# Three matmuls into an unread PSUM bank, ahead of the down projection of a one-token attention and gated MLP block

## The chip, the cores and the metric

The kernel runs on one core of a Trainium2 chip. The metric is device time in microseconds (us). The kernel before took 656.71 us, the median of three runs (656.64 to 656.9).

## What is computed

One token (512 values) passes through a layer norm, a grouped-query attention over a cache of 65,536 positions (32 query heads, 8 key/value heads of 128 values), a residual sum, a second layer norm, a gated MLP of width 1792 and a second residual sum. All inputs are bf16.

```python
q = layernorm(x) @ wq                          # 32 heads of 128
p = softmax(q . k_cache * 128**-0.5)           # 65536 positions, 4 query heads per kv head
h = x + (p . v_cache) @ wo                     # 4096 -> 512
n = layernorm(h)
h2 = h + (sigmoid(n @ w_gate) * (n @ w_up)) @ w_down   # 512 -> 1792 -> 512
```

The two caches are 268 MB of the 282.33 MB that the profile shows as read.

## The kernel before, in words

The program is written out by hand for each engine: `op(engine, function, waits, name)` appends one instruction to the list of its engine, and `emit` gives each name that somebody waits for a semaphore count. An instruction of a list runs behind all those ahead of it in the same list; what is not in `waits` is not waited for. An `op` without a name and without waits, as in the diff, neither waits nor raises a semaphore.

The cache streams through SBUF (`ring`) in large DMAs, all issued by SyncE (SP) in one order: for each of the eight heads a piece of K, a piece of V, and so on; then `w_o`, the last pieces of V, `w_gate`, `w_up`, and last `w_down` in three pieces (rows 0 to 8, 9 to 12, and 13 of fourteen, L362 to L365). VectorE (DVE) transposes the K blocks (L522), TensorE (PE) makes the scores and the sums over V (L434), ScalarE (ACT) the exponentials (L568).

After the last head comes a tail with one operation behind another:

- PE L641 makes the last four rows of the output projection in columns, DVE L824 adds `x` to give `hT`, and L392 to L404 with PE L395 make the mean and the reciprocal deviation (`rstd`, GpSimd L406).
- DVE L825 makes `hc`, the centred column; DVE L827 makes `hz`, from which the residual is put back into a row later.
- PE L838 multiplies `hc` by `w_gate` and `w_up`: 32 matmuls with one column of weights, 448 moving columns each, four beside one another in strips of 32 columns of the array, into the PSUM banks GB (2) and UB (3).
- PE L843, the residual's matmul, writes `h` into the bank YB (5) and opens the sum there. Its operands are fp32, and the trace shows it as two records.
- ACT L845 (tanh), DVE L846, L848 and L851 make the gated values `hh` and their transpose `hhT`.
- PE L857 adds the product with `w_down` to YB: fourteen rows of four matmuls with 128 columns, each group of four in the four strips. The first matmul of each piece waits for that piece's DMA (`wd0`, `wd1`, `wd2`), the very first one for `hhT` too.
- DVE L861 and ACT L862 copy the result out, and two DMAs (L865, on SP and ACT) write it to HBM.

PSUM bank PO is number 4. The heads' sums over V are made in it; ACT L609 reads it for the last time at the end of the last head. `ident` is a 128x128 identity in bf16, made at the start. `ktw` holds transposed K blocks, later rows of `w_o`; its first 384 columns are rows of `w_o` at the place of the change.

The wait of the down projection:

```python
["hhT", "hhT0", f"wd{i}"] if r == r0 and g == 0 else ()
```

Of the kernel before, what the change touches and what calls it, by code (L numbers as in the profile page):

```python
# [29 lines left out]
PO = 4  # L30
# [5 lines left out]
class Prog:  # L36
# [14 lines left out]
    def op(self, eng, fn, deps=(), name=None, to=None, times=1):  # L51
        assert name is None or name not in self.where, name
        self.ops[eng].append(dict(fn=fn, deps=[d for d in deps if d], name=name, dma=None, to=to, times=times, part=self.part.get(eng)))
        if name:
            self.where[name] = (eng, len(self.ops[eng]) - 1)
# [160 lines left out]
def bass_sequential_preLN__gqa_block_cached__glu_gated_glu__decode_kernel(  # L216
# [22 lines left out]
    with ExitStack() as es:  # L239
        def sb(name, shape, dt):  # L240
            return es.enter_context(nc.sbuf_tensor(name, shape, dt))
# [7 lines left out]
        ident = sb("ident", [128, 128], bf16)  # L249
# [7 lines left out]
        ktw = sb("ktw", [128, NKT * CH + WH], bf16)  # L257
# [48 lines left out]
        def ps(bank, c0, c1, p0=0, p1=128):  # L306
            return PS[p0:p1, bank * 512 + c0: bank * 512 + c1]
# [5 lines left out]
        op, dma = P.op, P.dma  # L313
# [519 lines left out]
        for i, (nm, bank) in enumerate((("wg", GB), ("wu", UB))):  # L833
            at = W_AT[nm]
            for kt in range(4):
                for c in range(4):
# [3 lines left out]
                        rhs=ring[:, at + kt * FF + c * FG: at + kt * FF + (c + 1) * FG],  # L840
                        start=(kt == 0), stop=(kt == 3), tile_position=(0, 32 * c)),
                       ["hc"] * (kt == 0 and c == 0) + dep, f"gu{i}" if kt == 3 and c == 3 else None)
        op("pe", lambda e: e.matmul(ps(YB, 0, 128), lhsT=gsel[:, :], rhs=hz[:, :], start=True, stop=False, skip_group_check=True), ["hz"])  # L843

        op("act", lambda e: e.activation(sg[:, :], ps(GB, 0, FG), AF.Tanh, scale=rstd[1][:, 0:1]), ["gu0", "rstd.1"], "sg")  # L845
        op("dve", lambda e: e.tensor_scalar(sg2[:, :], sg[:, :], 1.0, rstd[1][:, 0:1], op0=ALU.add, op1=ALU.mult), ["sg"], "sg2")  # L846
# [5 lines left out]
        for i, (r0, r1) in enumerate(WD_SPLIT):  # L852
            for r in range(r0, r1):
                for g in range(4):
# [4 lines left out]
                        start=False, stop=(r == NF - 1), tile_position=(0, 32 * g), skip_group_check=True),  # L859
# [36 lines left out]
```

## Time and profile before

| | |
|---|---|
| time, median of 3 runs (lowest, highest) | 656.71 us (656.64, 656.9) |
| time of the profiled execution | 656.72 us |
| its span, first to last instruction | 655.4 us |
| mean granted TensorE clock | 0.783 |
| busy: PE, DVE, ACT | 397.5, 350.5, 43.1 us |
| DMA queue of SP, share of 16 engines | 99.6% |
| read from HBM | 282.33 MB, 431 GB/s over the span |

Busy times overlap, so they do not add up to the span. The row of the DMA queue says that the 16 DMA engines had packets of it under way nearly throughout. The granted clock is the share of full speed that TensorE's clock gate let through; 0.5 and 1 are the two values it takes here over a stretch. A granted clock of one stretch comes from the view that cuts the span into windows.

### The profile page before, as it was taken

What the parts mean: (1) busy time and instruction counts of PE and PEld (TensorE: products, weight loads), DVE (VectorE), ACT (ScalarE), POOL (GpSimd) and SP (SyncE); (2) the same over time, 40 slices, a digit from 0 to 9 for tenths busy, and PEclk for the clock granted to TensorE, in tenths of its full rate; (3) what the DMA queues carried; (4) which work ended last, traced back from release to release, by engine and by line L of the source; (5) the groups of instructions that cost most, each with busy time, mean ns of one, the idle gap of its engine ahead of it and who ended that gap; (6) DMA issues with size and microseconds to landing.
All of it is one profiled execution on the core that took longest, in us unless ns stands there. A gap on an engine that the chain in (4) does not pass through costs nothing.

```text
span 655.4 us, 6173 instructions
## 1 busy us (share of the span) xinstructions
PE 397.5 (61%) x2317; PEld 66.0 (10%) x1549; DVE 350.5 (53%) x426; ACT 43.1 (7%) x114; POOL 3.6 (1%) x18
## 2 busy tenths in 40 slices
PE   2788672937548393764828467383855728285465
PEld 1100010110101000010100101010010101001122
DVE  3398853819266290935719184481917548092202
ACT  1100200020000200002000200002000020001101
POOL 1000000000000000000000000000000000000000
PEclk9789795877959587795968869596786969778656
DMA  9999999999999999998999999999999989999998
GB/s 390 442 432 464 424 408 448 448 436 396 448 448 448 424 408 448 448 448 384 448 448 448 428 404 448 448 448 408 424 448 448 448 384 448 448 448 424 427 404 361
DMA packets 6376, 282.33 MB, mean 431 GB/s; under 512 B 744, under 2 KB 872, under 8 KB 1256
## 3 DMA queue, kind: packets, MB, share of 16 engines
q1 hardware_dynamic: 6340, 282.33, 99.6%
q10 hardware_dynamic: 36, 0.00, 0.0%
HBM read 282.33 MB, written 0.00 MB: 431 GB/s over the span
## 4 chain that ended last, share of the span: by engine, by line
DMA 66%; DVE 31%; PE 1%; issue 1%; SPq 0%; PEldq 0%
DMA ring<-in_A_k_cache_dram 58%; DVE ktw L522 31%; DMA ring<-in_B_w_down_dram 5%; DMA ring<-in_A_v_cache_dram 4%; PE PS L434 1%; SPq L359 0%; PE PS L857 0%; SPq L364 0%; SPq L330 0%; DVE y_sb L861 0%; PEldq L171 0%
## 5 line engine op out<-in xcount | busy, mean ns | idle before, releaser
L522 DVE STREAM_TRANSPOSE ktw<-ring 128x1024 f32<-128x1024 f32 x256 | 291.7, 1208 | 166.6 <-DMA ring<-in_A_k_cache_dram 166.6
L434 PE MATMUL PS<-ktw 128*128 128x512 bf16 x1024 | 278.0, 421 | 163.4 <-DVE ktw L522 156.0
L434 PE MATMUL PS<-ring,PT_sb 128*32 x1024 | 85.7, 423 | 54.3 <-issue 46.2
L434 PEld LDWEIGHTS PS<-ktw 128*128 x256 | 26.2, 103 | 403.7 <-issue 240.3
L609 ACT ACTIVATE po_sb<-PS,rl 128x512 bf16<-128x512 f32 x8 | 5.5, 687 | 524.4 <-PE PS L434 524.4
L434 PEld LDWEIGHTS PS<-ring,PT_sb 128*32 x1024 | 20.7, 116 | 117.5 <-issue 116.1
L557 DVE TENSOR_REDUCE gmj<-PS 1x4 f32<-1x128 f32 x8 | 2.2, 279 | 53.3 <-PE PS L555 53.3
L529 DVE TENSOR_REDUCE M_sb<-PS 128x1 f32<-128x512 f32 x32 | 19.9, 683 | 19.3 <-PE PS L434 19.3
L568 ACT ACTIVATE P_sb<-PS,negmax 128x512 bf16<-128x512 f32 x32 | 21.5, 685 | 0.3
L578 DVE STREAM_TRANSPOSE PT_sb<-P_sb 128x512 bf16<-128x512 bf16 x32 | 19.9, 675 | 1.7 <-ACT P_sb L568 1.7
L434 PE MATMUL PS<-ktw,xz 128*8 x32 | 8.4, 429 | 3.6 <-DMA ktw<-in_A_wq_dram 3.6
L625 DVE TENSOR_TENSOR Lw<-O,blk_of 128x896 bf16<-128x896 bf16 (+1 forms) x2 | 1.4, 682 | 15.9 <-ACT O L615 15.9
L562 PE MATMUL PS<-one_f,gmrep 1*128 1x1 f32 x16 | 4.2, 332 | 5.0 <-DVE gmrep L559 5.0
L555 PE MATMUL PS<-identf,gm 128*1 128x128 f32 x16 | 4.3, 364 | 4.9 <-issue 2.8
L634 DVE CAST O<-PS 128x28 bf16<-128x28 f32 (+1 forms) x2 | 0.3, 173 | 12.7 <-PE PS L631 12.7
L480 DVE STREAM_TRANSPOSE qt<-qh 32x512 bf16<-32x512 bf16 x1 | 0.7, 700 | 11.1 <-ACT qh L477 11.1
L568 ACT ACTIVATION_READ_ACCUMULATOR P_sb<-PS,negmax 128x1 f32 x32 | 6.5, 203 | 0.0
L612 PE MATMUL PS<-sel_bf,po_sb 128*128 128x4 bf16 x32 | 2.1, 170 | 6.3 <-ACT po_sb L609 6.3
L495 ACT ACTIVATE PS<-zcol 128x512 f32<-128x512 bf16 x8 | 5.0, 622 | 0.0
L564 ACT ACTIVATE negmax<-PS 128x1 f32<-128x1 f32 x8 | 1.4, 171 | 54.5 <-PE PS L562 54.5
L583 PE MATMUL PS<-L_sb,lsel 128*128 128x4 f32 x16 | 2.5, 229 | 3.8 <-DVE PT_sb L578 3.8
L415 PE MATMUL PS<-xs,xpick 16*128 16x32 bf16 x1 | 0.2, 203 | 7.4 <-DMA xs<-in_A_x_dram 7.4
(88 smaller groups left out, 67.5 us busy)
## 6 DMA issues: line engine op xcount, KB each, us to landing
ring<-in_A_k_cache_dram SPq DMA_DIRECT2D x4, 4096.0 KB, 35.0
ring<-in_A_v_cache_dram SPq DMA_DIRECT2D x1, 5120.0 KB, 30.0
ktw<-in_A_wq_dram SPq DMA_DIRECT2D x1, 4096.0 KB, 12.2
ktw<-in_A_wo_dram SPq DMA_DIRECT2D x1, 3584.0 KB, 18.3
ring<-in_A_v_cache_dram SPq DMA_DIRECT2D x1, 3072.0 KB, 36.8
ring<-in_B_w_gate_dram SPq DMA_DIRECT2D x1, 1792.0 KB, 23.8
ring<-in_B_w_up_dram SPq DMA_DIRECT2D x1, 1344.0 KB, 26.6
ring<-in_B_w_down_dram SPq DMA_DIRECT2D x1, 1152.0 KB, 29.6
```

The source lines that it names most:

```text
L434: return e.add_instruction(mybir.InstMatmult(name=nc.get_next_instruction_name(), engine=mybir.EngineType.PE, ins=[rhs, lhsT], outs=[e.low ...
L495: op("act", lambda e: e.activation(ps(PO, 0, 512), bass.AP(tensor=zcol, offset=0, ap=[[1, 128], [0, 512]]), AF.Copy), ["zcol"] if h == 0 e ...
L522: op("dve", lambda e, d=dst, sr=src: e.transpose(d, sr), deps, f"T{b}.{c}", to="T")
L529: op("dve", lambda e, u=u: e.tensor_reduce(M_sb[:, u % 4:u % 4 + 1], ps(u % NS, 0, 512), AX.X, ALU.max), [f"S{b}.{NC - NR + k}"], f"mx{u}" ...
L555: op("pe", lambda e: e.matmul(ps(MISC, 0, 128, 0, 1), lhsT=gm[:, :], rhs=identf[:, :], start=True, stop=True), [f"gm{h}"], f"gmT{h}", to="Q")
L557: op("dve", lambda e: e.tensor_reduce(gmj[:, :], ps(MISC, 0, 128, 0, 1).rearrange("p (i a c) -> p a i c", a=4, c=NC), AX.XY, ALU.max), [f" ...
L562: op("pe", lambda e: e.matmul(ps(MISC, 128, 129), lhsT=gmrep[0:1, :], rhs=one_f[0:1, 0:1], start=True, stop=True), [f"gmrep{h}"], f"neg{h}")
L568: op("act", lambda e, b=b: e.activation(P_sb[:, (b % 4) * 512:(b % 4 + 1) * 512], ps(b % NS, 0, 512), AF.Exp, bias=negmax[:, k:k + 1], sca ...
L578: op("dve", lambda e, b=b: e.transpose(PT_sb[:, (b % 4) * 512:(b % 4 + 1) * 512], P_sb[:, (b % 4) * 512:(b % 4 + 1) * 512]), [f"E{b}"], f" ...
L583: op("pe", lambda e: e.matmul(ps(MISC, 132, 136), lhsT=lsel[:, :], rhs=L_sb[:, :], start=True, stop=True), [f"PT{NR * h + NR - 1}"], f"l{h ...
L609: op("act", lambda e: e.activation(po_sb[:, :], ps(PO, 0, 512), AF.Copy, scale=rl[:, :]), [f"PV{h}.{NR - 1}", f"rl{h}"], f"po{h}", to="po")
L612: op("pe", lambda e, t=t: e.matmul(ps(OX, 0, 4), lhsT=po_sb[:, t * 128:(t + 1) * 128], rhs=sel_bf[:, 8 * t:8 * t + 8:2], start=(t == 0), s ...
```

## The change

Behind the residual's matmul (L843), three more matmuls are appended to PE's list, each with the identity as weights (128x128) and 384 columns of `ktw` as moving data, written to columns 0 to 383 of bank PO. Nothing reads the bank afterwards. They have no waits and no names. All else stands as before, with line numbers from L845 on higher by two.

```diff
         op("pe", lambda e: e.matmul(ps(YB, 0, 128), lhsT=gsel[:, :], rhs=hz[:, :], start=True, stop=False, skip_group_check=True), ["hz"])
+        for _ in range(3):
+            op("pe", lambda e: e.matmul(ps(PO, 0, 384), lhsT=ident[:, :], rhs=ktw[:, 0:384], start=True, stop=True, skip_group_check=True))
 
         op("act", lambda e: e.activation(sg[:, :], ps(GB, 0, FG), AF.Tanh, scale=rstd[1][:, 0:1]), ["gu0", "rstd.1"], "sg")
```

In the order of PE's instructions the only difference is one row, three matmuls of 128x384 between L843 and the first matmul of L857; DVE, ACT, GpSimd and SP keep theirs.

## The prediction, as it was put on record

> **What bounds the kernel now.** I read the chain of waits first, over the last 70 us, because the change sits in the last 6 us of the span.
>
> ```profile
> by line: DMA ring<-in_B_w_down_dram 54.2%; DMA ring<-in_A_v_cache_dram 44.3%; PE PS L434 11.6%; issue 5.5%; SPq L359 2.1%; PE PS L857 1.0%; SPq L364 0.8%; DVE y_sb L861 0.5%; PEldq L171 0.3%
> ...
> 622.80 30.34 DMA ring<-in_B_w_down_dram
> 653.15 0.04 issue
> 653.19 0.56 PE PS L857 x17
> 653.75 0.02 issue
> 653.78 0.28 DVE y_sb L861
> ```
>
> The end is set by a DMA: the second piece of w_down, issued at 622.80, lands at 653.15, and 0.04 us later PE does the rest of the down projection. None of gate, up, tanh or transpose is on this chain. Next the instructions in order of time around the change:
>
> ```profile
> 650.30 0.58 PE L843 MATMUL PS<-hz,gsel 128*128 128x128 f32 x2
> 650.42 0.92 DVE L848 TENSOR_TENSOR hh<-PS,sg 128x448 bf16<-128x448 f32 x1 [0.37 <-PE PS L838]
> 651.37 0.65 DVE L851 STREAM_TRANSPOSE hhT<-hh 128x448 bf16<-128x448 bf16 x1
> 652.07 0.51 PEld L857 LDWEIGHTS PS<-ring,hhT 128*32 128x32 bf16 x36 [1.38 <-DVE hhT L851]
> 652.07 0.68 PE L857 MATMUL PS<-ring,hhT 128*32 128x128 bf16 x36 [1.19 <-DVE hhT L851]
> 653.19 0.40 PEld L857 LDWEIGHTS PS<-ring,hhT 128*32 128x32 bf16 x20 [0.61 <-DMA ring<-in_B_w_down_dram]
> 653.19 0.53 PE L857 MATMUL PS<-ring,hhT 128*32 128x128 bf16 x20 [0.43 <-DMA ring<-in_B_w_down_dram]
> ```
>
> PE has two holes here: 1.19 us from the residual's matmul (650.30 + 0.58 = 650.88) to the first row of w_down, ended by hhT, and 0.43 us between the first 36 matmuls and the last 20, ended by the DMA. The three pieces are issued at 622.33, 622.80 and about 623.3; with the 29.6, 30.3 and 30.2 us to landing that the DMA view gives (shortest, longest, median) they land near 651.9, 653.15 and 653.5. So the last row, too, waits for data: the last matmul starts at 653.5 by the line's view and ends at 653.75.
>
> Last the granted clock, from the view by windows (columns: window, length, then busy us and count for PE, weight load, DVE, ACT and POOL, then the clock, DMA share, GB/s):
>
> ```profile
> 650.40:650.50 0.10, 0.10 (x1) 0.10 (x2) 0.08 (x1) 0.00 (x0) 0.00 (x0) 0.50 1.08 461
> 650.50:650.60 0.10, 0.10 (x1) 0.10 (x2) 0.10 (x1) 0.00 (x0) 0.00 (x0) 0.86 1.52 645
> 650.60:650.70 0.10, 0.10 (x2) 0.09 (x1) 0.10 (x1) 0.00 (x0) 0.00 (x0) 1.00 0.87 369
> 650.70:652.00 1.30, 0.19 (x2) 0.00 (x0) 1.27 (x2) 0.00 (x0) 0.00 (x0) 1.00 0.93 386
> 652.00:653.70 1.70, 1.19 (x56) 0.84 (x56) 0.02 (x1) 0.00 (x0) 0.00 (x0) 1.00 0.55 210
> ...
> 653.90:654.00 0.10, 0.00 (x0) 0.00 (x0) 0.10 (x1) 0.10 (x1) 0.00 (x0) 0.71 0.00 0
> ```
>
> The clock goes from 0.50 to 1.00 inside the residual's matmul (0.86 on average in that tenth: at 650.53) and back at 653.94 (0.71: 42% of that tenth still at 1). All of w_down already runs at 1.00 in this execution. The column of GB/s says the rest: the stream runs near 400 GB/s until w_down is in.
>
> **The change part by part.** It removes nothing and moves no DMA, no wait and no other engine's instruction. It adds three weight loads of 128x128 bf16 and three matmuls of 384 columns behind L843, in the 1.19 us hole.
>
> Weight load: 0.103 us by the group of L434's loads of the same shape; the later two can lie beside the matmul ahead of them.
>
> Matmul at clock 1.00: thirteen 128x512 matmuls of L434 stand in 2.98 us from 127.50 (that stretch is at 1.00), and one of them takes 0.377 us on the mean, so one follows another after (2.98 - 0.38)/12 = 0.217 us. For 384 columns that is 0.163. The array is then taken for 0.10 + 3 x 0.163 = 0.59 us: from 650.88 to 651.47, or 0.60 before w_down starts at 652.07. Cost on the path: 0.
>
> Matmul at clock 0.50: the weight loads of L838 come in fours at 647.92, 648.29, 648.66, 649.04, one four per 0.373 us of 448 columns; 384 columns give 0.32, so 0.10 + 0.96 = 1.06 us, to 651.94. That still ends 0.13 us ahead of hhT. Cost: 0.
>
> What if the cover is smaller than this? Behind the three stands only L857 on PE; nobody but the two copies out of YB waits for it. If the first row were late, it would be late by nothing up to 0.43 us, the second hole, at clock 1.00. With all three exposed the ends are: 0.59 - 0.43 = 0.16 us at clock 1.00; at 0.50, 1.06 us less a hole of which w_down at half clock leaves 0.16 (nine fours at 0.373 x 128/448 = 0.107 us are 0.96 us, to 653.03, against 653.19), so 0.9. I take 0, because both rows put the end of the three ahead of hhT.
>
> Effect on DVE's L848 and L851, which run beside the three: they read banks 3 and SBUF, the three write bank 4. The trace shows PE running beside DVE at many places, not this pair. A slow-down of the two (1.57 us) by a quarter would be 0.39 us and stay inside the 0.43; a gain there would be worth nothing, since the DMA ends later. I take 0.
>
> Effect on the clock: w_down at 1.00 cannot become faster. At 0.50 it would end later: the second piece's four fours run from 653.19 to 653.62, the last row's to 653.73, plus the 0.21 us by which a matmul of L838 (0.58) outlasts its spacing (0.373): 653.94 against 653.75, so 0.19 us. That is all that a clock can give or take here: 0 to 0.19 us, 0.03% of the time.
>
> A rule that bears on this: "TensorE: Matmul & The Clock Gate" in the Trainium skill (Part 1, The HAM clock gate) says that about 3.4 us of sustained work release the full clock, that the window of activity is free-running, and that an idle window takes the clock away again. The trace agrees with the length: 653.94 - 650.53 = 3.41 us at 1.00. By that rule fill-in matmuls are worth something where a gap lets the clock fall; here the 0.19 us above is the most it can be.
>
> **The sum.** 656.72 (profiled time) + 0 = 656.72; the profiled execution stands 0.01 above the median, so I predict 656.7. What lies around the span (656.72 - 655.4 = 1.3 us) is not touched.
>
> **The rivals.**
>
> 1. **The clock was lower in other executions, and the three raise it.** Where the switch to 1.00 falls against the kernel can differ between executions. Full work on PE runs from 647.22 to 650.88 now, 3.66 us; with the three it runs to 651.47 or 651.94, 4.25 to 4.7 us, so a stretch of 3.41 us fits in at more positions. If the median execution of before had w_down at 0.50, it would gain 0.19: 656.5. Against it: the profiled execution had 1.00 and took 656.72, the median. For it: the highest run is 656.9, 0.18 above. It would not reach 0.2%.
>
> 2. **Slower: PE's instructions come late.** Six more instructions move the 112 of w_down back in PE's stream. If the sequencer has to wait for code somewhere in them, PE stands idle with no wait to show for it. The longest gap of matmuls of L434 that ends in "issue" is 1.3 us; a stall of that size behind 653.19 is all exposed and gives 658.0, and ahead of 652.07 or in the 0.43 us hole it is hidden for that much: it decides from the point where it outlasts the hole. Against it: the tail from 644.6 on is straight code, and PE's waits from 643 to the end name no "issue" gap at all. "Runtime: NRT & Kernel Launch" in the Trainium skill (Instruction fetch mechanics) says that an engine's code is refilled in blocks of 256 instructions and that crossing into one is mostly hidden; no row here shows a crossing, and by that rule the sum would stay as it is.
>
> 3. **Slower a little: the clock is at 0.50 and the three lie on the path.** Half clock and hhT ready earlier than 651.94, or weight loads that do not overlap (3 x 0.103 in place of one: +0.21, so 652.15, 0.08 us past hhT). With the 0.19 above: 657.0. It is inside 0.2%.
>
> 4. **The stream runs at another rate.** The program is another one, and 282.33 MB at 431 GB/s set the time; a rate off by 0.3% gives 654.7 or 658.7. The three runs of before lie within 0.26 us, 0.04%, which speaks against it.
>
> That the three are not there at all, or stand elsewhere, is ruled out by the order of PE's instructions; if they cost nothing, the time cannot tell.
>
> **How the numbers follow.** A measurement of this kernel can tell about 0.2%, 1.3 us, from no change: 655.4 to 658.0. Chances: no change (656.45 to 656.95) 0.80; rival 1 (656.5) 0.06; rival 2 (658.0) 0.06, of which 0.04 over the bound; rival 3 (657.0) 0.03; rival 4 0.05, 0.02 faster and 0.03 slower. So faster 0.02, same 0.91 (0.80 + 0.06 + 0.02 + 0.03), slower 0.07. Range 656.3 to 657.2: below, the clock's 0.19 under the lowest run (656.64) is 656.45, and I leave 0.15 for a median of few runs; above, rival 3 with the 0.19 that the highest run lies over the median. The fully exposed 0.9 us at half clock and rivals 2 and 4 (0.11) are left out.
>
> **What would show it.** In the profile after: three records of L845 starting at 650.9 after L843 and ending by 651.6 (clock 1.00) or near 652.1 (0.50); the first row of w_down still ended by hhT, 0.05 us after it; a hole ended by DMA w_down ahead of the last 20; the same 0.6 us from the landing to the last matmul. Wrong would be: w_down's first row following the three without a gap while the DMA's hole is gone, an "issue" gap inside L859, w_down at 0.50 throughout, or a landing later than 31 us after its issue.

## The result and the profile after

| | before | after |
|---|---|---|
| median (lowest to highest, 6 runs each) | 656.81 us (656.35 to 657.08) | 660.24 us (660.09 to 660.69) |
| profiled execution | 656.72 us | 660.19 us |
| its span | 655.4 us | 655.4 us |
| time less span | 1.3 us | 4.8 us (4.8 to 5.3 in the six runs) |

After to before is 1.0053, 95% interval 1.0042 to 1.0063: slower by 3.4 us, outside the range. The span has not changed at all. All of the loss lies outside the span, ahead of the first instruction or behind the last.

The profile's first lines for the kernel after: six records more (three loads, three matmuls), the same span.

```profile
span 655.4 us, 6179 instructions
## 1 busy us (share of the span) xinstructions
PE 396.2 (60%) x2320; PEld 67.0 (10%) x1552; DVE 350.3 (53%) x426; ACT 43.1 (7%) x114; POOL 3.6 (1%) x18
```

The instructions of the kernel after in order of time, around the change (start, us, engine, line, operation, count, idle before):

```profile
650.32 0.80 PE L843 MATMUL PS<-hz,gsel 128*128 128x128 f32 x2
...
650.91 1.17 PE L845 MATMUL PS<-ktw,ident 128*128 128x384 bf16 x3
...
652.09 0.88 PEld L859 LDWEIGHTS PS<-ring,hhT 128*32 128x32 bf16 x36 [0.71 <-DVE hhT L853]
652.09 1.65 PE L859 MATMUL PS<-ring,hhT 128*32 128x128 bf16 x56
653.20 0.40 PEld L859 LDWEIGHTS PS<-ring,hhT 128*32 128x32 bf16 x20 [0.23 <-DMA ring<-in_B_w_down_dram]
653.80 0.27 ACT L864 ACTIVATE y_sb<-PS 33x128 bf16<-33x128 f32 x1 [4.21 <-PE PS L859]
```

This execution had clock 0.50 through the three matmuls and w_down up to 653.0, and 0.89 on average from there to 653.8; w_down ended 0.02 us later than before all the same (ACT's copy starts at 653.80, before at 653.78). The loads of the last 20 still wait for the DMA.

### The profile page after: what moved, and what is told of

It reads as the page before. It is cut to its first block, busy times and chain, and to the rows that moved or that the text cites. A ratio compares the mean times of both kernels' runs of the same rounds, so it can differ in the third digit from the quotient of the medians.

```text
span 655.4 us, 6179 instructions
## 1 busy us (share of the span) xinstructions
PE 396.2 (60%) x2320; PEld 67.0 (10%) x1552; DVE 350.3 (53%) x426; ACT 43.1 (7%) x114; POOL 3.6 (1%) x18
## 4 chain that ended last, share of the span: by engine, by line
DMA 63%; DVE 31%; PE 4%; issue 1%; SPq 0%; ACT 0%
DMA ring<-in_A_k_cache_dram 58%; DVE ktw L522 31%; DMA ring<-in_A_v_cache_dram 6%; PE PS L434 2%; PE PS L838 0%; PE PS L859 0%; PE PS L845 0%; SPq L330 0%; PE PS L843 0%; PE PS L641 0%; ACT po_sb L609 0%; PE PS L395 0%; SPq L349 0%; DVE Lw L625 0%; DVE y_sb L863 0%
## 5 line engine op out<-in xcount | busy, mean ns | idle before, releaser
L434 PE MATMUL PS<-ring,PT_sb 128*32 x1024 | 84.2, 416 | 55.5 <-issue 46.9
```

The costliest lines, as they stand in the source:

```text
L434: return e.add_instruction(mybir.InstMatmult(name=nc.get_next_instruction_name(), engine=mybir.EngineType.PE, ins=[rhs, lhsT], outs=[e.low ...
```

## The experiments

My first theory: PE's program got longer by six instructions, and somewhere outside the span PE waits for code (A). The rival: what the three matmuls do (columns, bank, clock) costs something outside the span (B).

**Work or length.** `tiny3` puts three matmuls of one column in the same place, `mm1` and `mm2` one and two of 384 columns, `no_row8` keeps all three and drops a row of w_down's product.

```diff
# tiny3
+        for _ in range(3):
+            op("pe", lambda e: e.matmul(ps(PO, 0, 1, 96, 97), lhsT=zcol[:, :], rhs=zcol[:, :], start=True, stop=True, tile_position=(0, 96), skip_group_check=True))
# mm1, mm2: as the change, with range(1) and range(2)
# no_row8: the change, and in the loop of L859
+                if r == 8:
+                    continue
```

> Before, with three matmuls of one column and one weight column (zeros, 128x1) in place of the three of 384 columns: the same six instructions more on PE, next to no work in the array. Theory A (the 3.4 us are paid outside the span because PE's program got longer, whatever the instructions do): about 660.2. Theory B (the 3.4 us come from what the big matmuls do: 384 columns, a dirtied bank, a clock left in another state at the end): about 656.8. The span is 655.4 by both.

> One matmul of 384 columns in place of three, two instructions more on PE than before. Theory A, if the cost is a step at some length of the program: either 656.8 or 660.2, nothing between. Theory B, or a cost per instruction: about 658.0, a third of 3.4 us more than before.

> Two matmuls of 384 columns, four instructions more on PE. Theory A with a step: 656.8 or 660.2, and no less than with one matmul. Theory B, or a cost per instruction: about 659.1.

> The changed kernel with its three matmuls, but with the ninth row of w_down's product left out (part of the output sum is missing): eight PE instructions fewer, so two fewer than before the change. Theory A: back to 656.8, within 0.2. Theory B: 660.2, since the three matmuls still run.

| run | PE instructions against before | time, us (lowest to highest) | time less span |
|---|---|---|---|
| no_row8 | -2 | 656.69 (656.36 to 657.03) | 1.3 |
| before, same chip | 0 | 656.78 (656.48 to 657.14) | 1.3 |
| mm1 | +2 | 657.05 (656.68 to 657.56) | 1.6 to 1.7 |
| mm2 | +4 | 660.03 (659.83 to 660.59) | 4.4 to 5.0 |
| tiny3 | +6 | 660.37 (660.2 to 660.79) | 4.8 to 5.3 |

B falls twice: one-column matmuls cost as much as 384 columns (tiny3), and the three big ones cost nothing once the program is shorter (no_row8). It is a step in the length between +2 and +4. At +2 the time itself cannot be told from before (ratio 1.0003, interval 0.9993 to 1.0012), but time less span is 0.3 us longer: 1.60 to 1.68 in its ten runs, 1.28 to 1.38 in the nineteen of before.

**Which side of the span, and the branch hint.** All of PE's list stands in a body with a hint at its head and a branch back to the head at its end that is never taken (L179 to L192, `HINTED`). `late_before` and `late_after` add 5.4 us of DVE work behind PE's last matmul; `nohint_before` and `nohint_pad` take PE out of `HINTED`, which removes the hint and the never-taken branch together; below, "without the hint" means without both.

```diff
# late_before, late_after
+        for i in range(8):
+            op("dve", lambda e: e.transpose(hhT[:, 32:32 + FG], hh[:, :]), [f"late{i - 1}" if i else "y"], f"late{i}")
-        op("dve", lambda e: e.tensor_copy(y_sb[0:33, :], ps(YB, 0, 128, 0, 33)), ["y"], "ysb0")
+        op("dve", lambda e: e.tensor_copy(y_sb[0:33, :], ps(YB, 0, 128, 0, 33)), ["late7"], "ysb0")
# nohint_before; nohint_pad besides with range(5) in the change
-HINTED = ("pe", "dve", "act")
+HINTED = ("dve", "act")
```

> The kernel before, with eight more transposes of 128x448 on DVE, one behind the other, between the last matmul and DVE's copy of the result (about 8 x 0.65 to 0.7 us, so the span becomes some 5.5 us longer, about 661). PE has been done for that long when the program ends. Both theories on where the 3.4 us lie: time less span stays 1.3 us; this is the other half of the next run.

> The changed kernel with the same eight transposes. Theory End (PE waits for code at the end of its own program, behind its last matmul, and the program's end waits for PE): PE can do that beside the transposes, so time less span falls from 4.8 to 1.3 us and the time equals that of the kernel before with the transposes. Theory Start (the code is brought in ahead of the first instruction, or all engines are held): time less span stays 4.8 and the time is 3.4 us above it.

> The kernel before without the branch hint and the never-taken branch back around PE's program (PE is taken out of HINTED; three real instructions fewer). Theory Hint (the hint is what brings back the first code block in time, and the longer program defeats it): time less span rises to about 4.8, the time to 660.2. Theory Length alone (only the count decides): 656.8.

> Without the hint, and with five of the 384-column matmuls in place of three, so that PE's program is as long as the changed kernel's. Theory Hint: about 660.2, the same as without hint and short. Theory Length alone: 660.2 too, but 3.4 us above the short one without hint.

Measured: late_before 661.98 (span 660.6, time less span 1.3 to 1.4), late_after 665.64 (span 660.5, 4.7 to 5.1): PE's 5 us of leisure do not hide the cost, so theory End in this form falls. Without the hint the short program takes 657.93 and the long one 657.72, both with time less span 1.3: no step. Both theories that I had written down there fall, too; it takes the length and the hinted branch together. The hinted branch is worth having where the program is short: without it the short one is 1.1 us slower (657.93 against 656.87, ratio 1.0015, interval 1.0006 to 1.0025), all of it in the span (656.2 to 657.0 over ten runs, 655.0 to 656.1 with it over eighteen).

**Which place counts.** Three ways of lengthening, and a stretch of code long enough to bring the place where the step arises, a boundary in the code, into the program itself (`extra` is the one-column matmul of tiny3):

```diff
# behind2 (late_behind20: range(20), with late_before's transposes), behind the hinted branch
             self.nc.switch_bb(end)
+            if e == "pe":
+                for _ in range(2):
+                    self.extra(eng)
# head2, near the head of PE's list
+        for _ in range(2):
+            op("pe", lambda e: e.matmul(ps(PO, 0, D // XR), lhsT=xpick[:, :], rhs=xs[:, :], start=True, stop=True))
# mm2_pull: mm2, and ahead of the hint's target
+            if e == "pe":
+                o = self.ops[e].pop(0)
+                put(e, eng, o, waits_of(e, o, {}, {}, False))
```

> The kernel before with two one-column matmuls (four instructions) behind the never-taken hinted branch, at the very end of PE's program: the program is as long as the one with two 384-column matmuls (660.0), but the body between the hint's target and the branch is as long as before. Theory End place (what decides is where PE's last code, and what the runtime runs after it, comes to lie): 660.0 to 660.4. Theory Branch (what decides is where the hinted branch stands, or how long the body is): 656.8.

> Two small matmuls (32 columns, four instructions) near the head of PE's list, 640 us ahead of the tail, where PE waits for data; all later code moves up by four instructions. Theory Length or place of any kind inside the body: 660.0 to 660.4. If it were the tail's own code that matters: 656.8.

> The kernel with two 384-column matmuls (660.0), with PE's first matmul and its waits moved ahead of the hint's target: the body is as short as with one matmul or shorter, the program's length, the place of the branch and of the end unchanged. Theory Body length (distance from the branch back to its target): 656.8 to 657.1. Theory place or length of the whole: 660.0.

> The kernel before with the eight late transposes on DVE and twenty one-column matmuls (40 instructions) behind the hinted branch at the end of PE's program, where PE has some 5 us until the program ends. If the boundary that is passed lies within these 40 instructions, PE waits for code there beside DVE's transposes. Theory End place with an exposed wait only behind the common end: time less span 1.4, time about 662.0. Theory that the wait for code falls ahead of the first instruction, or behind the end whatever the place: 665.6.

Measured, on another chip on which the kernel before takes 656.75: 659.93 (659.54 to 660.55), 660.37 (659.92 to 660.83), 659.83 (659.6 to 660.61), so the cost comes wherever the instructions are put, behind the branch too, and a shorter body does not remove it: what counts is where the end of PE's program comes to lie. late_behind20, longer by 40, takes 661.89 (661.86 to 661.92), time less span 1.3: the cost is gone from outside the span. Its trace shows where it went, in PE's rows in order of time:

```profile
653.34 0.32 PEld L872 LDWEIGHTS PS<-zcol 128*1 128x1 bf16 x6
653.42 0.31 PE L872 MATMUL PS<-zcol 128*1 128x1 bf16 x5
...
657.36 0.51 PE L872 MATMUL PS<-zcol 128*1 128x1 bf16 x15 [3.62 <-issue]
657.36 0.41 PEld L872 LDWEIGHTS PS<-zcol 128*1 128x1 bf16 x14 [3.71 <-issue]
```

Six weight loads and five matmuls come before the gap. So between the eleventh and the twelfth instruction behind the branch PE stands still for 3.62 us, and no semaphore explains it ("issue"). These matmuls have no waits. Here DVE's transposes cover it.

**The changed kernel itself, the exact step, and the hint again.** In the first two the three 384-column matmuls stay; seventeen one-column ones stand behind the branch, with and without the late transposes. `mm2_kept` is longer by three. `late_nohint_behind22` passes the same place without the hint, twenty-two matmuls behind PE's list.

```diff
# late_after_behind17, after_behind17: the change, and behind the hinted branch
+            if e == "pe":
+                for _ in range(17):
+                    self.extra(eng)
# mm2_kept
+        op("pe", lambda e: e.matmul(ps(PO, 0, 384), lhsT=ident[:, :], rhs=ktw[:, 0:384], start=True, stop=True, skip_group_check=True))
+        op("pe", lambda e: mm_at(e, ps(PO, 0, 384), e.lower_ap(ident[:, :]), e.lower_ap(ktw[:, 0:384]), True, 128, kept=True))
# late_nohint_behind22: late_before, HINTED = ("dve", "act"), and
                 (hinted if e in HINTED else run)(e, eng)
+                for _ in range(22 if e == "pe" else 0):
+                    self.extra(eng)
```

> The changed kernel, its three 384-column matmuls in place, with the eight late transposes and seventeen one-column matmuls behind the hinted branch, so that the boundary lies inside PE's own program, ahead of the common end. Theory (a wait of 3.6 us for code at a fixed place of PE's program, exposed only behind the common end): an issue gap of about 3.6 us between the one-column matmuls, time less span 1.3, time 661.9, as without the three. Rival (the three matmuls themselves cost something outside the span as well): above 662.5.

> The same without the late transposes: PE has only 1.65 us (653.75 to 655.4) to hide the wait in. Theory: the gap of 3.6 us shows behind 653.8, PE ends near 658, and the span ends there in place of 655.4, while time less span is back at 1.3: about 659.3, 0.9 less than the changed kernel. Rival: 660.2, as the changed kernel.

> Two 384-column matmuls, the second with the weights kept, three instructions more than before: the one length between the two that were tried (two more: 657.05, four more: 660.03). Theory of a boundary: either 657.1 to 657.5 or 660.0, time less span either about 1.7 or about 4.5. Rival, a cost that grows with each instruction from there: about 658.5.

> The late transposes and twenty-two one-column matmuls at the end of a PE program without the hint (480 real instructions, against 479 with the hint): the same boundary is passed in plain sequence. Theory Hint (the code behind the hinted branch is not brought in ahead of time because of the hint): no issue gap over 0.5 us between the one-column matmuls. Rival (every passage of this boundary waits, hint or not): the gap of 3.6 us is there too. The time is about 663 in either case, since DVE's transposes cover it.

Measured: 661.82 (661.7 to 662.21), 659.36 (659.25 to 659.59), 660.49 (660.16 to 660.93) and 663.02 (662.79 to 663.45); before on the same chip 656.96 (656.39 to 657.24). Time less span is 1.3, 1.5 to 1.6, 4.7 to 5.2 and 1.3.

With the three matmuls in place and the gap covered, late_after_behind17 is as fast as late_before (661.82 and 661.98): nothing of the cost sticks to the three. Its gap is 3.55 us:

```profile
653.52 0.19 PE L875 MATMUL PS<-zcol 128*1 128x1 bf16 x2
657.26 0.51 PE L875 MATMUL PS<-zcol 128*1 128x1 bf16 x15 [3.55 <-issue]
```

The kernel after_behind17, without cover, shows the gap in PE's rows:

```profile
653.52 0.13 PEld L873 LDWEIGHTS PS<-zcol 128*1 128x1 bf16 x3
653.53 0.19 PE L873 MATMUL PS<-zcol 128*1 128x1 bf16 x2
657.30 0.51 PE L873 MATMUL PS<-zcol 128*1 128x1 bf16 x15 [3.58 <-issue]
```

In both it falls behind five instructions (three loads, two matmuls) in place of eleven: the six that the change adds have pushed the code on by six, and the boundary has stayed where it was. In after_behind17 the span itself grows, to 657.8, and the kernel is still 0.9 us faster than the shorter one of the change (659.36 against 660.24). mm2_kept puts the step between +2 and +3. And late_nohint_behind22 runs through:

```profile
654.72 0.73 PE L871 MATMUL PS<-zcol 128*1 128x1 bf16 x22
```

Twenty-two in one piece, no gap: the place costs nothing when PE comes to it without the hint.

**What the DMA records show.** I had taken these gaps for a wait for code without a record of it. The profile has one: a DMA queue of the kind "instruction" (q8; the other queue of that kind, q14, has packets only before the first instruction, in every trace). The DMA view of the kernel after, from 655.4 to 664 us, so behind its span, has one packet of 16,384 bytes:

```profile
q8 instruction: 1, 0.02, 0.7%
```

The same stretch of the kernel before has none:

```profile
DMA packets 0, 0.00 MB, mean 0 GB/s; under 512 B 0, under 2 KB 0, under 8 KB 0
```

The page of late_behind20 has it inside the span, that of late_nohint_behind22 two:

```profile
q8 instruction: 1, 0.02, 0.0%
q8 instruction: 2, 0.03, 0.0%
```

| runs | where the packet of 16,384 bytes starts | time less span, us |
|---|---|---|
| before, no_row8, late_before | none | 1.3 to 1.4 (one run of before 1.5) |
| mm1 | none | 1.6 to 1.7 |
| after, tiny3, mm2, mm2_kept, behind2, head2, mm2_pull, late_after | 2.0 to 2.5 us behind the end of the span (after: 657.48) | 4.4 to 5.3 |
| late_behind20, late_after_behind17 | 654.99 and 655.03, inside PE's gap | 1.3 to 1.4 |
| after_behind17 | 654.66, inside PE's gap | 1.5 to 1.6 |
| nohint_before, nohint_pad | 101.22 and 103.43 | 1.3 to 1.4 |
| late_nohint_behind22 | 103.69, and 655.51, after PE's last matmul | 1.3 to 1.4 |

So, by the profiled execution of each, every kernel that pays 3 us or more behind its span loads one packet of code there, and none of the others does. In late_behind20 PE's last row ahead of the gap ends at 653.73, the packet runs from 654.99 to 655.92, and PE goes on at 657.36.

Without the hint a packet of the same size comes some 550 us earlier, and that is also where the 1.1 us of the short program begin: VectorE starts on the next piece of K at 110.1 to 110.4 us in the three traces without the hint and at 108.9 to 109.6 in the fifteen with it. That the packet delays the stream is argued from this coincidence.

## Why the prediction was wrong, point by point

**The span: right.** "Cost: 0" at both clocks held. At 0.50 L843 took 0.80 us in place of 0.58 and the three ran from 650.91 to 652.08, where I had them leave the array at 651.94; w_down's first row came at 652.09, 0.05 us after hhT as before. PE's hole ahead of the last 20 closed, and the last matmul ended within 0.02 us of where it did before. In PE's rows this looks like the first sign that I had named for being wrong (the first row behind the three without a gap, the DMA's hole gone). It is not: PEld's rows still have the first load released by hhT and the last 20 by the DMA, and the row fills the hole because w_down ran at the lower clock. Rival 1, a clock raised by the three, does not show: this execution had the lower clock at that place with the three in it, and its span is 655.4 too.

**The step that failed:** "What lies around the span (656.72 - 655.4 = 1.3 us) is not touched." It went from 1.3 to 4.8 us, because PE's program is six instructions longer and a packet of code is now loaded behind the end of the span, at 657.48, where the kernel before loads none. I had taken the part outside the span for a constant, and had read the hint (L179 to L192) as something that the change leaves alone.

**Rival 2 had the right cause in the wrong place, at the wrong price.** I looked for late code inside the tail and found no "issue" gap from 643 us to the end of before, which was true: the load lies behind the end. The price was taken from the longest "issue" gap of a loop, 1.3 us; the wait behind the hinted branch is 3.6. And I argued with sequence ("straight code"), and left the hinted branch at its end out. The chance of 0.06 rested on rows inside the span, and nothing there tells how near to the step the end of PE's program stands: three instructions are enough.

**The page on code loading.** "Runtime: NRT & Kernel Launch" in the Trainium skill (Instruction fetch mechanics) says that code is refilled in blocks of 256 instructions, in sequence, and that a crossing is mostly hidden. The runs agree where there is no hint (no gap in late_nohint_behind22) and disagree where there is one (3.58 and 3.62 us). The measurement decides: in this program the load of code behind the hinted branch is not hidden, unless another engine's work covers it.

**What the runs leave open.** That PE waits for the packet is read from its place inside the gaps; the packet's record does not name the engine that it is for. Behind the span of the changed kernel the packet can be seen, but no instruction that waits for it. That the cost lies behind the common end of the engines, not ahead of the first instruction, follows from the packet's time and from late_after, where 5.4 us of other work do not hide it. Why the code is loaded early without the hint and late with it is not shown, nor which of the two, the hint or the never-taken branch, does it: no run removes only one. Why time less span is 0.3 us longer at +2, where no packet is loaded, is not settled. Whether DVE's and ACT's programs, which carry the same hint, have such a step was not tried.

## What to carry to other kernels

Compare time and span first. When the time moves and the span does not, the engines' rows do not hold the cause; the DMA view of the stretch behind the span may, and the length of the programs is the first thing to vary (one-column matmuls add instructions with next to no work). Here three instructions pushed the end of PE's program past a place from which on one more packet of code is loaded, and with the hinted branch that cost 3.5 us; it was found by adding and removing instructions anywhere in that engine's list. A wait for code can be moved: put where another engine's work covers it, it cost nothing.

## What the runs showed of the hardware that I had not expected

- Three more PE instructions (mm2_kept) cost 3.5 us, six with next to no work 3.6 (tiny3); two could not be told from none in the time. Forty more cost nothing where 5.4 us of DVE work lie beside them (late_behind20).
- Behind a hinted branch that is not taken, PE stood still for 3.55 to 3.62 us at a fixed place of its code, and one instruction packet of 16,384 bytes was loaded in that time; without the hint and its branch PE did not stop there.
- The same load shows in the DMA records behind the span: at 657.48 us in the changed kernel, whose span ends at 655.4.
- The hinted branch makes the short program 1.1 us faster (656.87 against 657.93), so it pays as long as the end of the program stays on the near side of that place.
